# Windowed attention into a gated feed-forward on one core: a new opening list, last hidden slices over whole token tiles, and a first output pass in two spans

## Chip, core and metric

The kernel runs on one core of a Trainium2 chip. The metric is the device time of one execution in microseconds (us), lower is better; where several executions were timed, the median counts. "The profile" is one execution taken with the hardware profiler; its times count from its first instruction. The engines are TensorE (PE in the profile, with its weight loads as PEld), VectorE (DVE), ScalarE (ACT), GpSimd (POOL) and SyncE (SP), and each works through its own instructions in order.

## The reference

```python
# q, k, v: (8 batches, 8 heads, 576 positions, 64), float32
scores = q @ k.T / sqrt(64)
rel = pos[:, None] - pos[None, :]
scores = where((rel >= 0) & (rel < 64), scores, -1e9)
attn = exp(scores - max(scores)); attn = attn / (sum(attn) + 1e-9)
x = (attn @ v).transpose(0, 2, 1, 3).reshape(4608, 512)
h = x @ w_in                      # w_in: 512 x 2048
out = (h * cos(h)) @ w_out        # w_out: 2048 x 512, out: 4608 x 512 float32
```

## The kernel before

The 4608 tokens are cut into nine tiles of 512 (`MT`). For each tile the feed-forward half runs on TensorE as 16 slices of 128 hidden columns (four matmuls of 128x512 per slice, line 445), each followed by a sine on ScalarE (cos h = sin(h + pi/2)) and a product on VectorE that writes the gated slice `gT`; then the output pass (line 607) forms four blocks of 128 tokens, 16 matmuls each. The attention for later batches is pumped in between these matmuls by a plan of due times (`at`, `pump`), so TensorE is given a single long stream.

Tile 0 is different. Nothing can be hidden behind an earlier tile, so everything up to its output pass is issued in the order of one list written out by hand, `FIRST`. A word of it is a step with its arguments and, at the end, the engine (a ScalarE, d VectorE, p GpSimd). The steps are, with p a pair of heads and g a half of the tile's 512 tokens:

- `ld.*` issues a load from the GpSimd queue: q and k of a head pair, v by chunks of 128 positions, `wA`, `wB`, `wC` three pieces of w_in (columns 0 to 512, 512 to 1280, 1280 to 2048), `q1b`, `k1b` the next batch's q and k, `wO`, `wP`, `wR` three pieces of w_out (slices 0 to 8, 8 to 12, 12 to 16). The very first q and k come over the SP queue in float32 and are cast by `cq`, `ck`.
- `io`, `id`, `mkd` build a ramp, the identity and the masks; `mka` casts the masks to bfloat16.
- `tq`, `tk` transpose q and k of a pair on TensorE (line 217); `pq`, `pk` copy them from PSUM to SBUF.
- `s` scores (a mask product, line 318, and eight blocks, line 308), `m` the row maxima (VectorE, line 327), `e` four exponentials (ScalarE, line 342), `i` reciprocals of the sums (VectorE), `n` the normalised weights (GpSimd or VectorE, line 356), `w` their transposes (TensorE, line 365), `c` the copy of these (VectorE).
- `z` copies halves of v to where the shifted blocks want them; `v.a.g` multiplies the weights by v for pairs 2a and 2a+1 (line 402), `x.a.g` copies the result to `xT`.
- `h.i.part` is half of a slice product (line 422): for i from 0 to 7 token half 0, for i from 8 to 15 token half 1, always two hidden slices 2(i mod 8) and 2(i mod 8)+1, with head pairs 0 and 1 in part 0, 2 and 3 in part 1. `sin.i` is its sine (line 428), `g.i` its product (line 433).
- `TQ`, `TK`, `EQ`, `EK` transpose and copy q and k of batch 1. `tb` loads ScalarE's sine table.

The PSUM banks of the scores turn through `S_FIRST`, those of the slices through `H_FIRST`, so `h.0` to `h.4` take the banks of the last five score groups, and `h.4.0` the bank that the last exponentials, `e.3.1`, read. The output pass of tile 0 goes through the hidden slices in three spans for both token blocks e = 0 and 1, so that slices which come late are asked for late:

```python
spans = ((0, 8), (8, 12), (12, 16)) if mt == 0 else ((0, n_ff),)
for lo, hi, e in [(lo, hi, e) for lo, hi in spans for e in range(2)]:
```

Block e = 0 ends in bank O1, which VectorE copies out, block e = 1 in O0, which ScalarE copies out; the next two blocks need the same banks.

Of the kernel before, what the change touches and what calls it, by code (L numbers as in the profile page):

```python
# [9 lines left out]
def _safe_warn(msg, *a, **kw):  # L10
# [6 lines left out]
ALU = mybir.AluOpType  # L17
# [46 lines left out]
def kernel(  # L64
# [9 lines left out]
    nc = tc.nc  # L74
# [5 lines left out]
    n_ff = d_ff // 128  # L80
    MT = 512
# [11 lines left out]
    w_in_sb = const.tile([128, PAIRS, d_ff], BF16, name="w_in")  # L93
# [9 lines left out]
    st = {}  # L103
# [39 lines left out]
    def load_heads(name, b, p0=0, n=PAIRS):  # L143
        if (name, b) not in st:
            st[name, b] = rows[name][b % 2][:, 0:PAIRS * RC * D].rearrange("p (a x) -> p a x", a=PAIRS)
        src = {"q": q, "k": k}[name][b, 2 * p0:2 * p0 + 2 * n]
        nc.gpsimd.dma_start(out=st[name, b][:, p0:p0 + n],
                            in_=src.rearrange("(a h) (p c) d -> (h p) a (c d)", h=2, c=RC))

    def load_first(name):  # L150
        st["f", name] = of = moe.tile([128, 2, d_model], F32, tag="out", name=name + "_f32", bufs=3)
        st["f", name] = of = of.rearrange("p a f -> p (a f)")[:, 0:RC * D]
        nc.sync.dma_start(out=of, in_={"q": q, "k": k}[name][0, 0:2].rearrange("h (p c) d -> (h p) (c d)", c=RC))

# [259 lines left out]
    def first_half(i, part):  # L414

        if part == 0:
            st["h0", i] = bank(H_FIRST[next(h_turn)], "h_ps").rearrange("p (e t) -> p e t", e=2)
        half = slice(MT // 2 * (i // 8), MT // 2 * (i // 8 + 1))
        for e in range(2):
            for ks in range(2 * part, 2 * part + 2):  # L420
                ff = 2 * (i % 8) + e
                nc.tensor.matmul(out=st["h0", i][:, e], lhsT=w_in_sb[:, ks, ff * 128:ff * 128 + 128],  # L422
                                 rhs=st["xT", 0][:, ks, half], start=ks + e == 0, stop=ks == PAIRS - 1,
                                 skip_group_check=True)

    def first_sin(i):
        st["sin", i] = moe.tile([128, MT], F32, tag="sin", name="sin", bufs=4)
# [2 lines left out]
    def first_gate(i):  # L430
        if not st["gT"]:
            st["gT"] = [moe.tile([128, 2, MT], BF16, tag="gT", name="gT", bufs=n_ff // 2 + 2) for _ in range(n_ff // 2)]
        nc.vector.tensor_tensor(out=st["gT"][i % 8][:, :, MT // 2 * (i // 8):MT // 2 * (i // 8 + 1)], in0=st.pop(("h0", i)),
                                in1=st.pop(("sin", i)).rearrange("p (e t) -> p e t", e=2), op=ALU.mult)

    def exp_table():
        nc.scalar.activation(small, small, AF.Exp, scale=0.0)
# [42 lines left out]
    n = n_first  # L480
# [54 lines left out]
    for name in ("q", "k"):  # L535
# [2 lines left out]
    exp_table()  # L538
    loads = {name + str(p): (load_heads, name, 0, p, 1) for name in ("q", "k") for p in range(1, PAIRS)}
    loads.update({f"v{c}": (load_v, 0, c) for c in range(4)})  # L540
    loads.update(wA=(load_w_in, 0, 512), wB=(load_w_in, 512, 1280), wC=(load_w_in, 1280, 2048),
                 q1b=(load_heads, "q", 1), k1b=(load_heads, "k", 1),
                 wO=(load_w_out, 0, 8), wP=(load_w_out, 8, 12), wR=(load_w_out, 12, 16))

# [25 lines left out]
    for mt in range(n_mt):  # L570
        base = mt * T
        gT = st["gT"] = [] if mt else st["gT"]
# [8 lines left out]
        for ff in range(n_ff) if mt else ():  # L581
# [4 lines left out]
            sin = moe.tile([128, MT], F32, tag="sin", name="sin", bufs=4)  # L586
# [3 lines left out]
            e = ff % 2  # L590
# [2 lines left out]
                exp_table()  # L593
            nc.vector.tensor_tensor(out=gt[:, e], in0=h_ps, in1=sin, op=ALU.mult)  # L594
            pump(base + ff)
        spans = ((0, 8), (8, 12), (12, 16)) if mt == 0 else ((0, n_ff),)
        for ms0 in range(0, MT // 128, 2):
            o_sb = moe.tile([128, 2, d_model], F32, tag="out", name="out_sb", bufs=3)
            o_ps = [bank(which, "out_ps") for which in (("O1",) if mt == n_mt - 1 and ms0 else ("O1", "O0"))]
# [1 line left out]
            for lo, hi, e in [(lo, hi, e) for lo, hi in spans for e in range(2)]:  # L601
# [4 lines left out]
                for ff in range(lo, hi):  # L606
                    nc.tensor.matmul(out=o_ps[e], lhsT=gT[ff // 2][:, ff % 2, ms * 128:ms * 128 + 128],  # L607
                                     rhs=w_out_sb[:, ff], start=ff == 0, stop=ff == n_ff - 1)
# [39 lines left out]
```

## Time and profile before

| | us |
|---|---|
| median of 3 runs | 301.59 (301.36 to 302.14) |
| the profiled execution, its own time | 301.93 |
| its span, first to last instruction | 300.1 |

| engine | busy us | share of the span |
|---|---|---|
| TensorE matmuls | 289.9 | 97% |
| TensorE weight loads | 148.1 | 49% |
| VectorE | 221.5 | 74% |
| ScalarE | 234.0 | 78% |
| GpSimd | 171.9 | 57% |

In a timeline row the columns are the start, the time from the first start to the last end of the merged instructions, engine, line, operation and tiles, shapes, how many, and in brackets how long the engine had been idle before and what released it. In a row of a table by stretches the columns are the stretch and its length, the busy time of each engine with its number of instructions, the granted TensorE clock, the share of the DMA engines and GB/s. In a row of the DMA view the last columns are how many transfers, the size of one and the time from issue to landing. The 1.83 us between the profiled time and its span lie outside the first and last instruction.

### The profile page before, as it was taken

To read this page: it belongs to the slowest core of one execution; us is meant where nothing else is said; L and a number is where in the kernel's file an instruction comes from. 1 tells how busy PE (TensorE), PEld (TensorE's weight loads), DVE (VectorE), ACT (ScalarE), POOL (GpSimd) and SP (SyncE) were. 2 spreads that over 40 slices of the span, in tenths; PEclk is the share of its full clock that TensorE was granted. 3 is DMA by queue.
4 is the path that set the end of the run, shared out by engine and by line. 5 is a ranking of instruction groups with operands and counts; after the bars stand their busy time and mean duration, and the time that the engine had idled before them with its cause. 6 is when DMAs were issued, how large, how long until landed. Compare 5 with 4: busy or idle time off the path is not lost.

```text
span 300.1 us, 8095 instructions
## 1 busy us (share of the span) xinstructions
PE 289.9 (97%) x2762; PEld 148.1 (49%) x2762; DVE 221.5 (74%) x852; ACT 234.0 (78%) x781; POOL 171.9 (57%) x202
## 2 busy tenths in 40 slices
PE   3899999999999999999999999999999999999996
PEld 2678744544454445444544454445444444454443
DVE  4899888689867897689678967896789678136701
ACT  4997899778997799879987998799879987016600
POOL 8997356994899278945994689549704610000000
PEclk9999999999999999999999999999999999999999
DMA  8999999999999999999999999999993480011011
GB/s 165 178 198 210 207 163 124 128 146 151 227 178 141 156 225 172 134 163 215 122 159 163 233 156 164 158 232 152 159 188 129 91 175 17 2 72 71 0 70 70
DMA packets 165929, 44.01 MB, mean 147 GB/s; under 512 B 155008, under 2 KB 161152, under 8 KB 165888
## 3 DMA queue, kind: packets, MB, share of 16 engines
q0 software_dynamic: 99360, 18.06, 77.8%
q1 hardware_dynamic: 66384, 25.24, 47.3%
q8 instruction: 21, 0.34, 0.5%
q10 hardware_dynamic: 144, 0.20, 0.2%
q14 instruction: 20, 0.16, 0.2%
HBM read 36.70 MB, written 9.44 MB: 154 GB/s over the span
## 4 chain that ended last, share of the span: by engine, by line
PE 90%; DVE 3%; ACT 2%; POOL 2%; issue 1%; DMA 1%; SPq 0%; DVEq 0%
PE out_ps L607 38%; PE h_ps L445 37%; PE h_ps L422 5%; PE o_ps L383 3%; PE s_ps L308 3%; POOL w L356 1%; ACT e L342 1%; DVE s L331 1%; DMA k_f<-in_k_dram 1%; PE out_ps L457 1%; PE tw_ps L365 1%; PE tk_ps L217 1%; DVE w L356 0%; PE tq_ps L217 0%; POOL v L116 0%
## 5 line engine op out<-in xcount | busy, mean ns | idle before, releaser
L607 PE MATMUL out_ps<-w_out,gT 128*128 128x512 bf16 x560 | 126.3, 379 | 0.5 <-DVE out_sb L116 0.5
L445 PE MATMUL h_ps<-xT,w_in 128*128 128x512 bf16 x512 | 112.0, 379 | 0.2
L594 DVE TENSOR_TENSOR gT<-h_ps,sin 128x512 bf16<-128x512 f32 x128 | 84.9, 688 | 30.1 <-ACT sin L591 30.1
L356 POOL TENSOR_TENSOR w<-e,rden 128x512 bf16<-128x512 f32 (+1 forms) x75 | 73.1, 986 | 54.7 <-DVE rden L349 52.6
L342 ACT ACTIVATE e<-s,negm 128x128 f32<-128x128 f32 x256 | 98.7, 388 | 0.2
L591 ACT ACTIVATE sin<-h_ps 128x512 f32<-128x512 f32 x128 | 73.8, 598 | 27.8 <-PE h_ps L445 26.7
L607 PEld LDWEIGHTS <-gT 128*128 128x128 bf16 x560 | 52.8, 98 | 61.3 <-issue 0.6
L445 PEld LDWEIGHTS <-w_in 128*128 128x128 bf16 x512 | 49.9, 98 | 59.1
L331 DVE CUSTOM_DVE_ANT_0 s<-s_ps,mask 128x128 f32<-128x128 f32 x256 | 57.9, 283 | 1.8 <-PE s_ps L308 1.6
L342 ACT ACTIVATION_READ_ACCUMULATOR e<-s,negm 128x1 f32 x256 | 48.2, 188 | 0.0
L174 POOL DMA_DIRECT2D v<-in_v_dram x40 | 34.1, 869 | 6.8 <-DMA w_out<-in_moe_w_out_dram 4.2
L116 ACT COPY out_sb<-out_ps 128x512 f32<-128x512 f32 (+1 forms) x18 | 10.2, 567 | 25.3 <-PE out_ps L607 19.6
L168 POOL DMA_DIRECT2D k<-in_k_dram x30 | 26.3, 882 | 4.5 <-DMA v<-in_v_dram 4.5
L168 POOL DMA_DIRECT2D q<-in_q_dram x30 | 25.4, 886 | 3.1 <-DMA w_out<-in_moe_w_out_dram 3.1
L116 DVE CAST xT<-o_ps 128x512 bf16<-128x512 f32 x28 | 18.2, 680 | 8.4 <-PE o_ps L383 8.2
L116 DVE COPY out_sb<-out_ps 128x512 f32<-128x512 f32 x18 | 12.3, 682 | 15.1 <-PE out_ps L607 15.1
L349 DVE RECIPROCAL rden<-den 128x4 f32<-128x4 f32 (+1 forms) x80 | 13.6, 171 | 10.2 <-ACT e L342 7.2
L331 DVE DVE_READ_ACCUMULATOR2_ANT negm<- 128x1 f32 x256 | 20.8, 81 | 0.0
L422 PE MATMUL h_ps<-xT,w_in 128*128 128x256 bf16 x128 | 15.5, 273 | 0.0
L422 PEld LDWEIGHTS <-w_in 128*128 128x128 bf16 x128 | 11.9, 98 | 1.5
L116 DVE COPY v<-v 64x1024 bf16<-64x1024 bf16 (+1 forms) x19 | 11.5, 605 | 0.4
L428 ACT ACTIVATE sin<-h_ps 128x512 f32<-128x512 f32 x16 | 9.1, 597 | 2.9 <-PE h_ps L422 2.9
(59 smaller groups left out, 185.8 us busy)
## 6 DMA issues: line engine op xcount, KB each, us to landing
out_dram<-out_sb SPq DMA_DIRECT2D x16, 512.0 KB, 7.8
v<-in_v_dram POOLq DMA_DIRECT2D x32, 128.0 KB, 5.9
q<-in_q_dram POOLq DMA_DIRECT2D x24, 128.0 KB, 9.3
k<-in_k_dram POOLq DMA_DIRECT2D x24, 128.0 KB, 7.8
w_in<-in_moe_w_in_dram POOLq DMA_DIRECT2D x2, 768.0 KB, 11.7
w_out<-in_moe_w_out_dram POOLq DMA_DIRECT2D x1, 1024.0 KB, 13.1
w_out<-in_moe_w_out_dram POOLq DMA_DIRECT2D x2, 512.0 KB, 15.6
wT<-w SPq DMA_TRANSPOSE x60, 5.0
```

Source lines behind the costliest of these rows:

```text
L116: {"a": nc.scalar.copy, "p": nc.gpsimd.tensor_copy}.get(engine, nc.vector.tensor_copy)(out, in_)
L168: nc.gpsimd.dma_start(out=st[name, b][:n, c].rearrange("p (h d) -> p h d", h=H), in_=src.rearrange("h p d -> p h d"))
L174: nc.gpsimd.dma_start(out=vt.rearrange("p (h d) -> p h d", h=H), in_=v[b, :, c * 128:c * 128 + n, :].rearrange("h p d -> p h d"))
L331: nc.vector.tensor_tensor_reduce(out=s[:, u], in0=s_ps[:, u], in1=mask[:, 2 - j % 2 if j else 0], scale=-scale if b else -1.0, scalar=BIG, ...
L342: nc.scalar.activation(e[:, u], s[:, u], AF.Exp, bias=negm[:, u:u + 1], scale=1.0 if n < n_first else -1.0, accum_out=den[:, u:u + 1])
L349: nc.vector.reciprocal(out=rden[:, 0:len(groups[n])], in_=den[:, 0:len(groups[n])])
L356: (nc.gpsimd if engine == "p" else nc.vector).tensor_tensor(out=w[:, 0:u], in0=e[:, 0:u], op=ALU.mult, in1=rden[:, 0:u].unsqueeze(2).to_br ...
L422: nc.tensor.matmul(out=st["h0", i][:, e], lhsT=w_in_sb[:, ks, ff * 128:ff * 128 + 128], rhs=st["xT", 0][:, ks, half], start=ks + e == 0, s ...
L445: nc.tensor.matmul(out=st["h", ff], lhsT=w_in_sb[:, ks, ff * 128:ff * 128 + 128], rhs=st["xT", mt][:, ks], start=start, stop=stop)
L591: nc.scalar.activation(sin, h_ps, AF.Sin, bias=math.pi / 2.0)
L594: nc.vector.tensor_tensor(out=gt[:, e], in0=h_ps, in1=sin, op=ALU.mult)
L607: nc.tensor.matmul(out=o_ps[e], lhsT=gT[ff // 2][:, ff % 2, ms * 128:ms * 128 + 128], rhs=w_out_sb[:, ff], start=ff == 0, stop=ff == n_ff - 1)
```

## The change

Three things change at once.

1. Six of the sixteen steps `h.i` of tile 0 (5, 6, 7, 13, 14, 15) no longer take one token half of two hidden slices, but all 512 tokens of one slice, 10 to 15; sine and product follow. Eight matmuls of 128x256 become four of 128x512 in each. The slices 0 to 9 stay in halves.
2. `wA` and `wB` are no longer columns 0 to 512 and 512 to 1280 for all head pairs, but columns 0 to 1280 for head pairs 0 and 1, and for 2 and 3. The output pass of tile 0 goes in two spans, slices 0 to 8 and 8 to 16.
3. The list `FIRST` is a new one. Engines of some steps change too: the casts `ck` to ScalarE and `mka` to VectorE, the copies `pq.0` and `pk.1` to VectorE, `pk.0` and `pq.1` to ScalarE, `x.1.0` and `c.3.1` to ScalarE, `x.0.1` to VectorE, and others.

```diff
+WHOLE = dict(zip((5, 6, 7, 13, 14, 15), range(10, 16)))
 FIRST = (
-    "ld.q1 ld.k1 io ld.q2 ld.k2 id mkd cq.a ck.d tq.0 ld.q3 tk.0 ld.k3 mka.a pq.0.a tq.1 pk.0.d s.0.0 "
-    "tk.1 s.0.1 pq.1.d ld.v0 tk.2 ld.v1 m.0.0 ld.wA pk.1.a ld.wB m.0.1 pk.2.d s.1.0 ld.v2 ld.v3 e.0.0 "
-    "i.0.0 n.0.0.p tq.2 m.1.0 ld.wC pq.2.d tq.3 s.2.0 tk.3 e.0.1 pq.3.d e.1.0 ld.q1b m.2.0 i.1.0 i.0.1 "
-    "n.1.0.d w.0.0 pk.3.a s.3.0 m.3.0 w.1.0 s.2.1 c.0.0.d s.1.1 c.1.0.d n.0.1.p z.0.p e.2.0 v.0.0 s.3.1 "
-    "e.3.0 i.2.0 m.2.1 e.2.1 m.1.1 n.2.0.p i.3.0 x.0.0.d n.3.0.p m.3.1 i.2.1 w.2.0 e.1.1 n.2.1.p c.2.0.d "
-    "h.0.0 w.3.0 e.3.1 c.3.0.d w.0.1 i.1.1 h.1.0 v.1.0 w.2.1 c.0.1.d n.1.1.p tb x.1.0.d h.2.0 c.2.1.d "
-    "i.3.1 n.3.1.d h.3.0 h.0.1 sin.0 h.1.1 w.1.1 ld.k1b z.1.d w.3.1 z.2.p c.1.1.d sin.1 h.2.1 c.3.1.d "
-    "h.3.1 v.0.1 ld.wO v.1.1 sin.2 h.4.0 h.4.1 g.0 x.0.1.a g.1 h.8.0 x.1.1.d g.2 h.9.0 h.8.1 sin.3 sin.4 "
-    "sin.8 h.9.1 ld.wP h.10.0 g.3 sin.9 h.11.0 h.10.1 sin.10 g.4 h.11.1 h.12.0 g.8 h.12.1 sin.11 h.5.0 "
-    "g.9 sin.12 h.5.1 TQ.0 g.10 sin.5 h.6.0 h.6.1 h.7.0 EQ.0.0.a g.11 g.12 h.7.1 sin.6 g.5 sin.7 TK.0 "
-    "h.13.0 EK.0.0.a h.13.1 EQ.0.1.d TQ.2 sin.13 g.6 g.7 h.14.0 EQ.2.0.a EQ.2.1.a h.14.1 EK.0.1.d TK.2 "
-    "sin.14 h.15.0 g.13 h.15.1 ld.wR EK.2.1.a sin.15 EK.2.0.d g.14 g.15 "
+    "ld.q1 cq.a ld.k1 ld.q2 io ld.k2 id mkd tq.0 ld.q3 ld.k3 ck.a tk.0 mka.d tq.1 pq.0.d pk.0.a pq.1.a "
+    "s.0.0 tk.1 m.0.0 e.0.0 s.0.1 ld.v0 pk.1.d ld.v1 m.0.1 s.1.0 ld.wA tq.2 s.1.1 i.0.0 m.1.0 ld.wB "
+    "pq.2.d tk.2 e.0.1 ld.v2 i.0.1 e.1.0 n.0.0.p ld.v3 n.0.1.p tq.3 m.1.1 pk.2.d tk.3 s.2.0 i.1.0 n.1.0.p "
+    "pk.3.a pq.3.d w.0.0 z.0.p s.3.0 e.1.1 m.2.0 c.0.0.d m.3.0 w.1.0 e.2.0 c.1.0.d ld.wC s.2.1 v.0.0 "
+    "m.2.1 i.1.1 i.2.0 x.0.0.d s.3.1 m.3.1 w.0.1 n.2.0.p e.3.0 n.1.1.p h.0.0 i.3.0 n.3.0.d c.0.1.d h.1.0 "
+    "e.2.1 w.2.0 h.2.0 c.2.0.d w.3.0 w.1.1 i.2.1 h.3.0 c.3.0.d e.3.1 c.1.1.d v.1.0 i.3.1 n.3.1.d h.4.0 "
+    "ld.q1b n.2.1.p x.1.0.a w.2.1 tb ld.k1b h.0.1 c.2.1.d w.3.1 z.1.d sin.0 h.1.1 c.3.1.a g.0 z.2.p h.2.1 "
+    "h.3.1 v.0.1 x.0.1.d ld.wO v.1.1 sin.1 x.1.1.a sin.2 g.1 ld.wP g.2 h.4.1 h.8.0 h.8.1 sin.3 h.9.0 "
+    "h.9.1 h.10.0 g.3 sin.4 sin.8 ld.wR h.10.1 g.4 h.11.0 sin.9 h.11.1 g.8 g.9 h.12.0 h.12.1 sin.10 TQ.0 "
+    "sin.11 g.10 sin.12 h.5.0 g.11 EQ.0.1.a EQ.0.0.d g.12 h.5.1 h.6.0 h.6.1 h.7.0 sin.5 TK.0 h.7.1 sin.6 "
+    "EK.0.0.d h.13.0 h.13.1 g.6 g.5 TQ.2 EK.0.1.a sin.7 sin.13 EQ.2.0.a EQ.2.1.a h.14.0 h.14.1 g.13 TK.2 "
+    "sin.14 g.7 h.15.0 EK.2.1.d EK.2.0.a h.15.1 g.14 sin.15 g.15 "
 )
...
-        for e in range(2):
+        for e in range(1 if i in WHOLE else 2):
             for ks in range(2 * part, 2 * part + 2):
-                ff = 2 * (i % 8) + e
-                nc.tensor.matmul(out=st["h0", i][:, e], lhsT=w_in_sb[:, ks, ff * 128:ff * 128 + 128],
-                                 rhs=st["xT", 0][:, ks, half], start=ks + e == 0, stop=ks == PAIRS - 1,
-                                 skip_group_check=True)
+                ff = WHOLE.get(i, 2 * (i % 8) + e)
+                nc.tensor.matmul(out=st["h0", i].rearrange("p e t -> p (e t)") if i in WHOLE else st["h0", i][:, e],
+                                 lhsT=w_in_sb[:, ks, ff * 128:ff * 128 + 128],
+                                 rhs=st["xT", 0][:, ks] if i in WHOLE else st["xT", 0][:, ks, half],
+                                 start=ks + e == 0, stop=ks == PAIRS - 1, skip_group_check=True)
...
+        if i in WHOLE:
+            to, of = st["gT"][WHOLE[i] // 2][:, WHOLE[i] % 2], of.rearrange("p e t -> p (e t)")
...
-    loads.update(wA=(load_w_in, 0, 512), wB=(load_w_in, 512, 1280), wC=(load_w_in, 1280, 2048),
+    loads.update(wA=(load_w_in, 0, 1280, 0, 2), wB=(load_w_in, 0, 1280, 2, 4), wC=(load_w_in, 1280, 2048),
...
-        spans = ((0, 8), (8, 12), (12, 16)) if mt == 0 else ((0, n_ff),)
+        spans = ((0, 8), (8, 16)) if mt == 0 else ((0, n_ff),)
```

More of the change, by code (lines that the diff above doesn't have):

```diff
@@ L432, in first_gate @@
             st["gT"] = [moe.tile([128, 2, MT], BF16, tag="gT", name="gT", bufs=n_ff // 2 + 2) for _ in range(n_ff // 2)]
-        nc.vector.tensor_tensor(out=st["gT"][i % 8][:, :, MT // 2 * (i // 8):MT // 2 * (i // 8 + 1)], in0=st.pop(("h0", i)),
-                                in1=st.pop(("sin", i)).rearrange("p (e t) -> p e t", e=2), op=ALU.mult)
+        to, of, sin = st["gT"][i % 8][:, :, MT // 2 * (i // 8):MT // 2 * (i // 8 + 1)], st.pop(("h0", i)), st.pop(("sin", i))
+        if i in WHOLE:
+            to, of = st["gT"][WHOLE[i] // 2][:, WHOLE[i] % 2], of.rearrange("p e t -> p (e t)")
+        else:
+            sin = sin.rearrange("p (e t) -> p e t", e=2)
+        nc.vector.tensor_tensor(out=to, in0=of, in1=sin, op=ALU.mult)
     def exp_table():
```

## The prediction

> **What bounds the kernel now.** I read the page first, then a table by stretches, then the timelines of the opening.
>
> ```profile
> span 300.1 us, 8095 instructions
> PE 90%; DVE 3%; ACT 2%; POOL 2%; issue 1%; DMA 1%; SPq 0%; DVEq 0%
> ```
> ```profile
> 5.00:20.50 15.50, 13.64 (x277) 9.76 (x276) 13.05 (x30) 13.21 (x68) 14.67 (x18) 1.00 1.43 182
> 20.50:37.50 17.00, 16.62 (x318) 13.73 (x317) 15.51 (x27) 13.85 (x26) 10.19 (x13) 1.00 1.22 209
> 37.50:58.00 20.50, 19.98 (x225) 9.87 (x224) 17.39 (x109) 19.04 (x85) 14.14 (x18) 1.00 1.38 129
> 58.00:284.00 226.00, 225.71 (x1856) 107.44 (x1855) 171.37 (x678) 184.41 (x600) 129.06 (x145) 1.00 1.33 147
> ```
>
> The chain that ended last is TensorE for 90%. From 58 to 284 us TensorE idles 0.29 us, and the change touches nothing there: what it does to the start of that stretch it does to the end. Before it TensorE idles 1.86 us (5 to 20.5), 0.38 (to 37.5) and 0.52 (to 58). These idles, slow or superfluous matmuls, and the time to the first work are all there is to win.
>
> **The opening, walked through the new list.** These rows give the durations: TensorE, then ScalarE, then VectorE.
>
> ```profile
> 5.33 0.69 PE L217 MATMUL tk_ps<-ident,k 64*64 64x64 bf16 x18 [0.31 <-DVE k L116]
> 6.43 0.61 PE L318 MATMUL s_ps<-mask,ident 128*128 128x256 bf16 x2
> 6.97 0.64 PE L308 MATMUL s_ps<-kT,qT 64*64 64x128 bf16 x8
> 15.37 0.41 PE L308 MATMUL s_ps<-kT,qT 64*64 64x128 bf16 x8
> 19.77 0.40 PE L365 MATMUL tw_ps<-ident,w 128*128 128x128 bf16 x4
> 20.00 1.91 PE L422 MATMUL h_ps<-xT,w_in 128*128 128x256 bf16 x16
> 23.16 0.76 PE L402 MATMUL o_ps<-wT,v 128*64 128x64 bf16 x32
> 23.85 6.29 PE L422 MATMUL h_ps<-xT,w_in 128*128 128x256 bf16 x56
> 36.49 0.41 PE L308 MATMUL s_ps<-kT,qT 64*64 64x128 bf16 x14
> 37.28 0.24 PE L308 MATMUL s_ps<-kT,qT 64*64 64x128 bf16 x2 [0.38 <-ACT sin L428]
> 37.46 2.76 PE L607 MATMUL out_ps<-w_out,gT 128*128 128x512 bf16 x12
> 57.56 13.34 PE L445 MATMUL h_ps<-xT,w_in 128*128 128x512 bf16 x61
> ```
> ```profile
> 3.61 0.67 ACT L116 CAST q<-q_f 128x576 bf16<-128x576 f32 x1 [1.36 <-DMA q_f<-in_q_dram]
> 8.66 0.37 ACT L342 ACTIVATE e<-s_ps,negm 128x128 f32<-128x128 f32 x1
> 10.04 0.39 ACT L342 ACTIVATE e<-s_ps,negm 128x128 f32<-128x128 f32 x1
> 12.82 0.68 ACT L116 COPY kT<-tk_ps 128x576 bf16<-128x576 bf16 x1
> 13.36 0.41 ACT L342 ACTIVATE e<-s_ps,negm 128x128 f32<-128x128 f32 x1
> 18.87 0.49 ACT L342 ACTIVATE e<-s_ps,negm 128x128 f32<-128x128 f32 x1
> 20.15 0.35 ACT L342 ACTIVATION_READ_ACCUMULATOR e<-s_ps,negm 128x1 f32 x1
> ```
> ```profile
> 4.82 0.46 DVE L116 CAST k<-k_f 128x576 bf16<-128x576 f32 x1
> 6.74 0.75 DVE L239 TENSOR_SCALAR qT<-tq_ps 128x576 bf16<-128x576 bf16 x1
> 7.65 0.69 DVE L327 TENSOR_REDUCE negm<-s_ps 128x4 f32<-128x512 f32 x1 [0.16 <-PE s_ps L308]
> 19.88 0.69 DVE L116 CAST xT<-o_ps 128x512 bf16<-128x512 f32 x1 [0.22 <-PE o_ps L402]
> ```
>
> *First scores.* The cast of k goes from VectorE (0.46) to ScalarE, where the same cast of q takes 0.67: `tk.0` starts at 5.53 instead of 5.33, and all behind it on TensorE up to the first scores shifts by 0.20. So `m.0.0` starts at 7.85, and `e.0.0`, which no longer has a copy of kT ahead of it on ScalarE, at 7.85 + 0.69 + 0.02 = 8.56 instead of 8.66. The mask cast, now on VectorE, and the ramp, now one load later on GpSimd, are covered: TensorE is busy with `tk.0` and `tq.1` meanwhile.
>
> *ScalarE's eight groups.* A group takes 1.38 (8.66 to 10.04), the last one 1.63 from its first start to its end (18.87 to 20.50), the copy `pk.3` 0.54 (12.82 to 13.36). New is one wait: `m.0.1` stands behind the copy `pk.1` on VectorE (some 0.7, as the qT copy) and ends near 10.12, 0.2 after ScalarE is free. Sum: 8.56 + 7 x 1.38 + 0.54 + 0.20 + 1.63 = 20.59, against 20.50 now. The other maxima I find in time, by as little as 0.2. VectorE's queue, with 0.61 from the start of a maximum to the next and 0.67 for a copy: `m.0.1` from 9.43 (when `s.0.1` is through), `i.0.0`, `m.1.0` from 10.3, `pq.2`, `i.0.1` at 11.7, `m.1.1` from 11.85, `pk.2` to 13.1, `i.1.0` (after `e.1.0`, whose first row starts at 11.52 and whose sums are there 1.5 later), `pq.3` from 13.3, `m.2.0` from 13.97, ended at 14.65. `e.2.0` can start at 10.14 + 3 x 1.38 + 0.54 = 14.82.
>
> *TensorE up to the second half.* By then the new list has put `h.0.0` to `h.3.0` and `v.1.0` through (ready near 20.4), and waits for `e.3.1` to free the bank of `h.4.0`. From 20.62: five steps `h` of 0.44 (four of the sixteen matmuls that take 20.00 to 21.75 in the row order above; `h.4.0`, `h.0.1` to `h.3.1`), two `w` of 0.23, `v.0.1` and `v.1.1` 0.69: 23.97. Then `h.4.1` to 24.41. `h.8.0` needs `x.0.1`, for which VectorE takes 0.69 after `v.0.1`: 24.55. In the kernel before the same point is 23.85 plus the eight matmuls of `h.4` at 0.111 (6.22 / 56): 24.74. Gain 0.19. `x.1.0`, now on ScalarE between the last exponentials and the sine table, puts `sin.0` off by its 0.6; the product `g.0` is then through near 23.8, before `h.8.0` wants its bank, so this costs nothing as long as TensorE is not more than 0.7 earlier than I have it.
>
> *Fewer matmuls.* 48 of 128x256 at 0.111 become 24 of 128x512 at 0.217 (13.27 / 61): 5.33 - 5.21 = 0.12, whole, because TensorE has no idle there. Sine and product keep their size, so ScalarE and VectorE gain nothing.
>
> *The end of the opening.* Now 14 of the 16 first scores of batch 1 run at 36.49, and the last two wait until 37.28 behind ScalarE: 0.38 idle, up to 0.58 counted by starts. In the new list the last copies of kT (`EK.2.1` now on VectorE, `EK.2.0` on ScalarE) still stand just ahead of `sin.15`. Bounds: the wait stays (0) or goes (-0.58). By my walk the ScalarE copy ends some 0.3 after TensorE asks, so I take -0.30.
>
> **The output pass of tile 0.** In rows of TensorE and VectorE:
>
> ```profile
> 46.02 0.33 PE L365 MATMUL tw_ps<-ident,w 128*128 128x128 bf16 x3
> 46.87 1.02 PE L607 MATMUL out_ps<-w_out,gT 128*128 128x512 bf16 x4 [0.52 <-DVE out_sb L116]
> 52.63 0.69 PE L383 MATMUL o_ps<-wT,v 128*64 128x64 bf16 x32
> ```
> ```profile
> 46.13 0.68 DVE L116 COPY out_sb<-out_ps 128x512 f32<-128x512 f32 x1
> ```
>
> Block e = 0 now ends only four matmuls and a transpose before bank O1 is wanted again, and VectorE, with maxima queued ahead, frees it 0.52 late. With two spans e = 0 ends one group of four earlier: eight matmuls, a transpose, twelve scores and another transpose lie between, about 2.4 us (3 to 4 groups at 0.87 and 0.2 to 0.3 for the rest) instead of 1.2. The copy then ends some 1.1 us before the bank is wanted. Bounds: 0 (another wait takes its place) and -0.68 (46.02 plus 0.17 of transposes to 46.87); I take -0.60, as the neighbours on VectorE keep their distances from TensorE.
>
> **Loads.** The order on the GpSimd queue stays the same, but `wC` and `q1b` are issued some 4 and 6 us later, behind norms and `z.0`. In the trace the transfers are a single backlog that never runs dry, so landings are set by bytes, which stay:
>
> ```profile
> 22.55 2.38 POOL L202 DMA_DIRECT2D w_out<-in_moe_w_out_dram  x3
> ```
> ```profile
> w_out<-in_moe_w_out_dram POOLq DMA_DIRECT2D x1, 1024.0 KB, 13.1
> ```
> ```profile
> w_out<-in_moe_w_out_dram POOLq DMA_DIRECT2D x1, 512.0 KB, 16.6
> ```
> ```profile
> 44.63 1.29 SPq L183 DMA_DIRECT2D v<-v  x2
> ```
> ```profile
> v<-v SPq DMA_DIRECT2D x1, 256.0 KB, 5.6
> ```
>
> The first piece of w_out lands at 22.55 + 13.1 = 35.65, the last (third issue, near 24.2) at 40.8. With the gains above the output pass starts at 37.46 - 0.19 - 0.12 - 0.30 = 36.85, and the two spans ask for the last piece after 16 + 4 matmuls, two score groups and a transpose, at about 42.2: in time by 1.4. The spread of batch 1's v lands at 45.3 + 5.6 = 50.9, and the products that read it, at 52.63 now, come at 52.63 - 1.21 = 51.4: also in time, but this caps any gain at 1.7. w_in's pieces by head pairs cost nothing: part 0 wants `wA`, part 1 `wB`, which is needed at 21.3 only.
>
> **Sum.** -0.19 - 0.12 - 0.30 - 0.60 = -1.21. On the profiled execution 301.93 - 1.21 = 300.72 (span 298.9). That execution stands 0.34 above the median, so for the median I say 301.59 - 1.2 = 300.4.
>
> **A rule against it.** The row of the first mask product shows 0.61 for two matmuls and the eight scores 0.64, later 0.41, while the granted clock stands at 1.00 from the start. The Trainium skill (TensorE: Matmul & The Clock Gate, Part 1: The HAM clock gate) says that TensorE runs at half rate until it has been busy for a window of about 3.4 us, whose phase is free. The durations agree that the start is slow, the clock column does not show it. The new list stretches the hole before `tk.0` and adds waits near 12 to 13 us; by that rule the fast rate could come one window later, which is the third rival.
>
> **The rivals.**
> - *Only the output pass pays.* The list is bound by the same exponentials (20.59 against 20.50), and my 0.2 us margins may be lost: then only about 0.6 stays, 301.0. For it: the loop ScalarE, reciprocal, copies, maximum, ScalarE is close everywhere. Against: TensorE has done two steps `h` more at 20.6.
> - *ScalarE and VectorE slip against each other, and it is slower.* Place: VectorE's queue from `i.1.0` to `m.3.0`. `i.1.0` waits for `e.1.0`, and behind it stand the copy `pq.3`, `m.2.0`, `c.0.0`, `m.3.0`, for which `e.2.0` and `e.3.0` wait. Beyond 0.2 us each delay there passes in full to ScalarE, to `h.4.0`, and to the end; TensorE, in order, can't go around it. The change loses from 1.21 + 0.2 = 1.4 us on. Two groups late by one group (1.38 x 2 = 2.8, less 0.2) make 300.4 + 2.6 = 303.0; one makes 301.6. Against: VectorE is idle for moments, so it can catch up.
> - *The fast rate comes 3.4 us later.* Score groups then cost 0.64 / 0.41 = 1.56 times as much. Of 3.4 us of TensorE work in 10 to 13.5 that is 3.4 x (1 - 0.41 / 0.64) = 1.2, of which the wait for `pk.2` hides about 0.6: 301.0.
> - *All goes well.* The score wait goes entirely and the output pass wins 0.68; the v spread caps it at 1.7: 299.9.
>
> **How the numbers follow.** Forecast 0.44 (its own range 300.0 to 300.8, from the bounds 0 and -0.58, 0 and -0.68), the best case 0.07, the output pass alone 0.20, slipping 0.20, the slow rate 0.09. A measurement tells about 0.3% (0.9 us) from no change: faster means under 300.69, slower over 302.49. The forecast is faster in about 0.42 of its 0.44, the best case wholly: 0.49. The second rival's milder half (0.04) and the two cases near 301.0 are the same, with the forecast's rest: 0.35. Slower 0.16. The range reaches from below the best case to between the two outcomes of slipping: 299.7 to 302.4.
>
> **What would show it.** Right: `e.0.0` near 8.6, `h.4.0` near 20.6 right after the last exponential, `h.8.0` near 24.6, the first L613 output matmul at 36.5 to 37.1, no idle at the first output matmul of the second pair of blocks. Wrong: ScalarE idle among its exponentials, scores or slices waiting for VectorE between 12 and 25 us, an output matmul waiting for w_out, or a products row (L384) waiting for the SP spread.

## The result, and the profile after

| | us |
|---|---|
| kernel after, median of 12 runs | 304.57 (302.27 to 307.24) |
| kernel before, median of 12 runs beside it | 301.94 (301.36 to 302.47) |
| ratio after / before | 1.0082, 95% interval 1.0062 to 1.0103 |
| profiled execution of after, its own time / span | 302.27 / 300.5 |

The change makes the kernel slower by 0.8%. The forecast was 300.4, and the time lies outside its range. The profiled execution is the quickest of the twelve, 2.3 us below their median, so it shows the loss at its smallest.

The kernel after by stretches (length, then busy time and records in brackets for TensorE, its weight loads, VectorE, ScalarE and GpSimd, then the granted clock, DMA share, GB/s):

```profile
5.00:20.50 15.50, 14.22 (x276) 10.14 (x276) 13.50 (x32) 13.34 (x68) 13.53 (x17) 1.00 1.40 187
20.50:37.50 17.00, 16.75 (x305) 11.37 (x301) 15.06 (x25) 14.79 (x27) 10.53 (x14) 1.00 1.22 209
58.00:284.00 226.00, 222.54 (x1825) 106.98 (x1851) 170.51 (x676) 183.80 (x599) 128.41 (x144) 1.00 1.35 146
```

TensorE has 0.58 us more busy time in the first stretch (14.22 against 13.64): the new list leaves it idle less. In the last row it seems to lose 3.2 us, but only 1825 matmul records are there, against 1856 before: most of that is records that are missing, and idle time can't be read from this row. It has to be read from the rows with a named wait. The timeline of TensorE in the kernel after (start, busy time, instruction, and in brackets the idle time before it and what ended it):

```profile
20.66 0.61 PE L423 MATMUL h_ps<-xT,w_in 128*128 128x256 bf16 x4
24.13 5.13 PE L423 MATMUL h_ps<-xT,w_in 128*128 128x256 bf16 x44
36.42 0.42 PE L309 MATMUL s_ps<-kT,qT 64*64 64x128 bf16 x16
36.77 2.76 PE L613 MATMUL out_ps<-w_out,gT 128*128 128x512 bf16 x12
45.50 1.03 PE L613 MATMUL out_ps<-w_out,gT 128*128 128x512 bf16 x3
56.81 13.34 PE L451 MATMUL h_ps<-xT,w_in 128*128 128x512 bf16 x60
86.11 1.01 PE L384 MATMUL o_ps<-wT,v 128*64 128x64 bf16 x52
88.05 0.38 PE L384 MATMUL o_ps<-wT,v 128*64 128x64 bf16 x12 [0.93 <-DMA wT<-w]
88.36 3.84 PE L451 MATMUL h_ps<-xT,w_in 128*128 128x512 bf16 x16
```

and the same place of the kernel before:

```profile
86.86 1.20 PE L383 MATMUL o_ps<-wT,v 128*64 128x64 bf16 x64
88.09 13.97 PE L445 MATMUL h_ps<-xT,w_in 128*128 128x512 bf16 x64
```

Up to the output pass the change does what it was forecast to do: the first output matmul comes at 36.77 (37.46 before), both waits are gone, tile 1's h starts 0.75 earlier. Then, at the products of tile 2, TensorE asks for w's transposes at 86.11, 0.75 earlier than before, and waits 0.93 us for the last of them: tile 2's h starts at 88.36, 0.27 later than before, and the span is 0.4 longer. These transposes are transfers from SyncE's queue (line 369). A list of the transfers issued from 75.3 to 82 us shows them (count, median from issue to landing), in the kernel before and after:

```profile
wT<-w SPq DMA_TRANSPOSE x4, 6.8
```
```profile
wT<-w SPq DMA_TRANSPOSE x4, 7.8
```

On SyncE they stand behind tile 0's two output stores (before, then after; the busy time here is that of issuing):

```profile
71.64 1.04 SPq L465 DMA_DIRECT2D out_dram<-out_sb  x2
76.41 6.40 SPq L368 DMA_TRANSPOSE wT<-w  x4
```
```profile
72.43 1.08 SPq L471 DMA_DIRECT2D out_dram<-out_sb  x2
75.66 6.12 SPq L369 DMA_TRANSPOSE wT<-w  x4
```

Issued 0.75 earlier, they take 1.0 longer, while the stores go out 0.8 later, so that 3.2 us instead of 4.8 lie between the stores and the first transpose. The chain of waits of the kernel after says the same: TensorE is 82% of it (90% before) and w's transposes by DMA 4%:

```profile
PE 82%; DVE 7%; DMA 5%; issue 2%; ACT 1%; POOL 1%; SPq 0%; DVEq 0%; POOLq 0%
PE h_ps L451 36%; PE out_ps L613 34%; PE h_ps L423 4%; DMA wT<-w 4%; PE s_ps L309 3%; DVE s L332 2%; PE o_ps L384 2%; DVE xT L117 1%; PE out_ps L463 1%; DMA k_f<-in_k_dram 1%; DVE negm L328 1%; DVE w L357 1%; ACT e L343 1%; DVE rden L350 1%
```

### The profile page after: what moved, and what is told of

It is laid out like the page before. It is cut to its first block, busy times and chain, and to the rows that moved or that the text cites. A ratio compares the mean times of both kernels' runs of the same rounds, so it can differ in the third digit from the quotient of the medians.

```text
span 300.5 us, 8008 instructions
## 1 busy us (share of the span) xinstructions
PE 287.7 (96%) x2703; PEld 146.0 (49%) x2738; DVE 220.9 (74%) x850; ACT 235.0 (78%) x783; POOL 170.8 (57%) x202
## 4 chain that ended last, share of the span: by engine, by line
PE 82%; DVE 7%; DMA 5%; issue 2%; ACT 1%; POOL 1%; SPq 0%; DVEq 0%; POOLq 0%
PE h_ps L451 36%; PE out_ps L613 34%; PE h_ps L423 4%; DMA wT<-w 4%; PE s_ps L309 3%; DVE s L332 2%; PE o_ps L384 2%; DVE xT L117 1%; PE out_ps L463 1%; DMA k_f<-in_k_dram 1%; DVE negm L328 1%; DVE w L357 1%; ACT e L343 1%; DVE rden L350 1%; POOL w L357 1%
## 5 line engine op out<-in xcount | busy, mean ns | idle before, releaser
L613 PE MATMUL out_ps<-w_out,gT 128*128 128x512 bf16 x542 | 123.5, 379 | 1.7 <-issue 1.3
L597 ACT ACTIVATE sin<-h_ps 128x512 f32<-128x512 f32 x128 | 73.8, 599 | 29.1 <-PE h_ps L451 28.0
L451 PEld LDWEIGHTS <-w_in 128*128 128x128 bf16 x512 | 49.9, 98 | 59.1
L423 PE MATMUL h_ps<-xT,w_in 128*128 128x256 bf16 (+1 forms) x101 | 15.6, 295 | 0.3 <-DVE xT L117 0.2
L343 ACT ACTIVATE e<-s_ps,negm 128x128 f32<-128x128 f32 x32 | 11.3, 439 | 1.3 <-DVE negm L328 1.2
L384 PEld LDWEIGHTS <-v 128*64 128x64 bf16 x512 | 9.1, 112 | 5.2 <-issue 4.7
```

Of the source, the lines that this page charges most:

```text
L343: nc.scalar.activation(e[:, u], s[:, u], AF.Exp, bias=negm[:, u:u + 1], scale=1.0 if n < n_first else -1.0, accum_out=den[:, u:u + 1])
L423: nc.tensor.matmul(out=st["h0", i].rearrange("p e t -> p (e t)") if i in WHOLE else st["h0", i][:, e], lhsT=w_in_sb[:, ks, ff * 128:ff * 1 ...
L451: nc.tensor.matmul(out=st["h", ff], lhsT=w_in_sb[:, ks, ff * 128:ff * 128 + 128], rhs=st["xT", mt][:, ks], start=start, stop=stop)
L597: nc.scalar.activation(sin, h_ps, AF.Sin, bias=math.pi / 2.0)
```

## The experiments

Each had the kernel before timed beside it; the interval is that of the ratio at 95%. "WHOLE" is the change's slices over all tokens.

| kernel | median us (range) | ratio to before |
|---|---|---|
| again: the kernel after | 303.70 (302.49 to 307.0) | 1.0070 (1.0035 to 1.0104) |
| list_only: before + new list | 303.47 (302.72 to 304.97) | 1.0057 (1.0037 to 1.0078) |
| rows_only: before + w_in by head pairs | 301.71 (301.41 to 303.33) | 0.9997 (0.9981 to 1.0013) |
| whole_spans: before + WHOLE + two spans | 302.28 (301.05 to 306.12) | 1.0014 (0.9989 to 1.0038) |
| after_late: after + 1.1 us of matmuls | 302.59 (301.99 to 308.19) | 1.0043 (1.0014 to 1.0073) |
| before_late: before + the same | 303.66 (302.48 to 303.88) | 1.0050 (1.0031 to 1.0068) |
| after_direct: after + 2 groups on TensorE | 301.69 (300.9 to 303.44) | 0.9995 (0.9979 to 1.0011) |
| ws_direct: whole_spans + the same | 301.37 (300.77 to 301.94) | 0.9981 (0.9968 to 0.9994) |
| after_store: after, stores early | 306.47 (304.7 to 307.78) | 1.0139 (1.0103 to 1.0176) |
| before_store | 306.32 (305.25 to 306.83) | 1.0137 (1.0113 to 1.0162) |
| ws_store | 306.56 (305.58 to 309.72) | 1.0164 (1.0126 to 1.0202) |
| ws_direct_store | 307.93 (305.44 to 308.5) | 1.0188 (1.0157 to 1.0219) |
| after_unstored: after, tile 0 not stored | 302.03 (301.33 to 302.61) | 1.0003 (0.9991 to 1.0016) |
| before_unstored | 302.00 (301.64 to 303.31) | 1.0011 (0.9998 to 1.0025) |
| after_half: after, 2nd store behind transposes | 301.29 (300.63 to 303.1) | 0.9983 (0.9969 to 0.9998) |
| ws_half: whole_spans + the same | 301.47 (300.9 to 303.06) | 0.9989 (0.9971 to 1.0006) |
| ws_direct_half: ws_direct + the same | 301.64 (300.94 to 304.41) | 1.0002 (0.9978 to 1.0025) |
| list_half: list_only + the same | 303.66 (302.12 to 305.85) | 1.0043 (1.0023 to 1.0062) |

**1. The parts of the change.** The kernel after once more, and its parts alone, each with its hunks of the change's diff: the new `FIRST`; the pieces of w_in; WHOLE with the two spans under the old list.

> The changed kernel once more, nothing edited. Theory A (the opening is faster, but the DMA transposes of w that tile 2's values product reads are behind a backlog of loads that does not move with TensorE, so TensorE waits for them, more or less long from execution to execution): the first output matmul again near 36.8 us, the product of tile 2's values (L384, near 88 us) again waits for a DMA transpose, by another amount; the longer the execution, the longer that wait or others of its kind; median 304 to 305. Theory B (the new shape of w_in's pieces disturbs the loads): the same here. Theory C (the TensorE clock alone varies): no waits for DMA, matmuls slow.

> The kernel before with the new list alone (w_in's pieces, half slices and three spans as before). Theory A: opening 0.5 us earlier, no total gain; a wait for a transpose of w in tile 1 or 2; 302 to 304. Theory B: nothing of the loads is changed in shape, so the gain of the opening stays: 301.2 to 301.6.

> The kernel before with w_in's first two pieces by rows of head pairs alone. Theory A: TensorE's opening stays, so the phase of TensorE against the loads stays: 301.6 to 302.3, as before. Theory B: 303 to 305 with its spread.

> The kernel before with the six whole slices and the two spans, the old list and w_in's old pieces. Theory A: the output pass of tile 0 ends about 0.7 us earlier and the transposes of w are waited for: no gain, 302 to 304. Theory B: the gain stays: 301.0 to 301.4.

The median of `again` (303.70) is a little below the 304 to 305 that was expected. Its profiled execution (307.0, the slowest of these eight runs) shows the loss at its largest. TensorE's timeline, then stretches of it:

```profile
56.35 3.84 PE L451 MATMUL h_ps<-xT,w_in 128*128 128x512 bf16 x17
70.04 0.64 PE L309 MATMUL s_ps<-kX,qX 64*64 64x128 bf16 x32 [0.35 <-DMA kX<-k]
87.44 0.44 PE L384 MATMUL o_ps<-wT,v 128*64 128x64 bf16 x16 [0.62 <-DMA wT<-w]
89.86 0.54 PE L384 MATMUL o_ps<-wT,v 128*64 128x64 bf16 x12 [1.98 <-DMA wT<-w]
90.33 16.75 PE L451 MATMUL h_ps<-xT,w_in 128*128 128x512 bf16 x64
```
```profile
86.00:90.00 4.00, 1.40 (x60) 1.15 (x61) 1.37 (x3) 2.62 (x5) 3.66 (x6) 0.89 1.72 168
90.00:94.00 4.00, 4.00 (x21) 1.60 (x19) 0.69 (x1) 0.00 (x0) 4.00 (x6) 0.50 2.34 154
94.00:98.00 4.00, 4.00 (x15) 1.64 (x14) 2.50 (x4) 2.55 (x5) 3.81 (x5) 0.75 2.17 166
```

Here tile 1's h starts at 56.35, just the 1.21 before the old 57.56 that the prediction summed up. Then TensorE waits 0.35 for batch 2's transposed k (`kX`) and 0.62 and 1.98 for w's transposes, and after that the clock is granted at half (0.50 from 90 to 94 us): tile 2's 64 matmuls take 16.75 instead of 13.97, another 2.8 us. The four transposes take 8.9 in this execution (7.8 in the first). So late transfers are paid twice here, and the two payments make up the whole loss: tile 2's h starts 2.24 later than in the kernel before and takes 2.8 longer, and the span is 5.1 longer (305.2 against 300.1). The Trainium skill (TensorE: Matmul & The Clock Gate, Part 1: The HAM clock gate) says that TensorE falls back to half rate after an idle window of about 3.4 us; the half rate agrees, the window is looked at below.

The pieces of w_in change nothing, so theory B falls, and the named waits for DMA speak against C. WHOLE with the two spans alone, under the old list, brings the whole gain ahead of tile 1 and loses half of it at the same place: in this execution (301.38, the third quickest of twelve that reach 306.12) tile 2's h starts 0.55 earlier than in the kernel before. TensorE's timeline in whole_spans:

```profile
36.55 1.69 PE L613 MATMUL out_ps<-w_out,gT 128*128 128x512 bf16 x7
56.35 1.90 PE L451 MATMUL h_ps<-xT,w_in 128*128 128x512 bf16 x8
87.23 0.38 PE L384 MATMUL o_ps<-wT,v 128*64 128x64 bf16 x12 [0.57 <-DMA wT<-w]
87.54 2.76 PE L451 MATMUL h_ps<-xT,w_in 128*128 128x512 bf16 x12
```

The new list alone loses 1.6 us and gains nothing, also not ahead of tile 1, against what was expected. Its profiled execution (302.72, the quickest of nine, 0.79 above that of the kernel before) has no wait for a transpose of w at tile 2, but a longer one at the last scores of the opening, 0.89 us instead of 0.38 (TensorE's timeline in list_only):

```profile
37.70 0.24 PE L308 MATMUL s_ps<-kT,qT 64*64 64x128 bf16 x2 [0.89 <-DVE gT L433]
```

That makes tile 1 start 0.42 later than in the kernel before; a wait of 0.21 for kX at 71.53 follows. Experiment 5 comes back to the list.

**2. TensorE put back, or the late transposes taken off the queue.** In two kernels, five overwritten matmuls (5 x 0.217 = 1.1 us) ahead of tile 1's h; in two others, two more of batch 2's head groups transposed on TensorE.

```diff
         def first(...):   # at the first head pair, before its four slices' matmuls
+            for _ in range(5 if (mt, ff) == (1, 0) else 0):
+                nc.tensor.matmul(out=st["h", ff], lhsT=w_in_sb[:, ks, ff * 128:ff * 128 + 128],
+                                 rhs=st["xT", mt][:, ks], start=True, stop=True)
```
```diff
-DIRECT = (0, 1, 2, 3, 4, 5, 8, 9, 16, 17, 26, 27)
+DIRECT = (0, 1, 2, 3, 4, 5, 8, 9, 14, 15, 16, 17, 26, 27)
```

> The kernel after with five extra 128x512 matmuls of TensorE (5 x 0.217 = 1.1 us, overwritten by the group behind them, so the output stays) at the start of tile 1's h, which puts tile 1 and all behind it back to where it lies in the kernel before. Theory A (the transposes by DMA of batch 2's w land late behind loads that do not move with TensorE; an earlier TensorE only waits for them, and long waits lower the clock): the extra work costs less than its 1.1, the median lies at 301.8 to 303.0, not above that of the kernel after, the waits for wT at tile 2's values shrink below 0.5 us in all, and single runs above 305 become rare. Theory C (the clock or the load order of the new list alone, whatever TensorE's phase): the extra work comes on top, 1.1 us above the kernel after, 304.6 to 305.7, with the same spread.

> The kernel before with the same five extra matmuls at the start of tile 1's h, as the price of the extra work where no transfer is late. In the kernel before TensorE takes tile 2's values without a wait, so by theory A the extra work costs up to its whole 1.1 us: 302.7 to 303.1. If it costs nothing (301.6 to 302.1), then a wait for a transfer, at tile 2 or behind it, binds the kernel before too, and anything gained ahead of it was lost from the start. Theory C says nothing against 303.0.

> The kernel after, where the w of two more head groups of batch 2 (pairs 2 and 3, whose transposes by DMA land last ahead of tile 2) is transposed on TensorE: eight more 128x128 transposes (8 x 0.1 = 0.8 us of TensorE) and their copies. Theory A: no wait for wT is left at tile 2's values, no halved clock behind it; the gain of the opening (0.7 to 1.2) stays, less the 0.8: 301.0 to 302.3, with single runs within 1 us of each other. Theory C: nothing changes but the added 0.8, 304 to 305.5.

> The kernel before with the whole-token slices and the two spans of the change, the old list and the old w_in pieces, and the two further head groups of batch 2 transposed on TensorE. Theory A: 1.2 us gained ahead of tile 1 and kept through tile 2, less 0.8 of transposes: 301.0 to 301.8, that is 0 to 0.9 below the kernel before, and no wait for wT at 84 to 90 us. Theory C, or a cost of the copies on VectorE that is larger than the wait: 302.3 or more, no better than the same kernel without the two groups (302.28).

1.1 us of extra work cost the kernel before 1.75 (303.66 against 301.91, more than expected), and the kernel after nothing: 302.59, less than the 303.7 and 304.57 that it took without. So by the medians TensorE only waits away what it gained. The 0.65 above the work itself is the opening's, as far as the profiled execution of before_late (303.82) shows: TensorE waits 0.61 at 6.40 us for the load of the second head pair's q, which it does not in the kernel before, and the second pair of output blocks starts at 47.70 instead of 46.87. But theory A's "shrink below 0.5" failed: in the profiled execution of after_late (305.66, the third slowest of twelve) the waits are as long as ever.

```profile
88.75 0.44 PE L384 MATMUL o_ps<-wT,v 128*64 128x64 bf16 x16 [0.59 <-DMA wT<-w]
91.44 0.38 PE L384 MATMUL o_ps<-wT,v 128*64 128x64 bf16 x12 [2.25 <-DMA wT<-w]
```

The landing is not a fixed time, then: TensorE asks for these products at 87.41, 0.55 later than in the kernel before, and still waits, since the transposes take 9.0 here. So an early TensorE is not all that makes them late; experiments 3 and 4 look for the rest. With two groups fewer by DMA the waits are gone and the loss with them. TensorE's timeline in ws_direct:

```profile
86.02 1.20 PE L384 MATMUL o_ps<-wT,v 128*64 128x64 bf16 x64
87.25 5.12 PE L451 MATMUL h_ps<-xT,w_in 128*128 128x512 bf16 x23
```

No wait, tile 2 starts 0.84 earlier than in the kernel before, and the range narrows to 300.77 to 301.94. The medians are theory A's forecast for both kernels (301.0 to 302.3, 301.0 to 301.8), and C's 304 falls. The runs of after_direct spread over 2.5 us, though, not over the 1 that was expected.

**3. Which traffic makes them late: the stores moved ahead.** Theory A1 blames tile 0's two output stores, A2 the loads of batch 3.

```diff
-        nc.sync.dma_start(out=out[r0:r0 + n * 128]...
+        (nc.sync if mt else nc.scalar).dma_start(out=out[r0:r0 + n * 128]...
-                at(base + T + 6 + ms0 / 2, store, o_sb, mt, ms0, 0, 2)
+                at(base + T + (6 + ms0 / 2 if mt else 1.5 * ms0 - 4), store, o_sb, mt, ms0, 0, 2)
```

> The kernel after, whose two stores of tile 0's output (2 x 512 KB, issued near 72 and 73 us from SyncE and landed near 80 and 81.5, just as the transposes by DMA for tile 2 are issued) are issued from ScalarE's queue near 53 and 57 us instead, where the DMA engines move least. Theory A1 (the stores are what the transposes stand behind): the transposes issued at 75 to 81 us land in 5 to 6.5 us instead of 7 to 9, no wait for wT is left at tile 2's values, and the gain of the opening shows: 300.6 to 301.5. Theory A2 (the transposes stand behind the loads of batch 3's q, k and v, the stores are beside the point): they still take 7 us and more, and the time stays at 302.3 to 304.6. If the earlier stores delay the transposes of batch 2's k, the scores at 70 us wait for kX instead, and the time is that of A2 or worse.

> The kernel before with the same two stores from ScalarE's queue, as the price of the move where no transpose is late. A1 and A2: 301.6 to 302.2, within 0.3 of the kernel before, as no wait of TensorE goes and ScalarE has room for two issues; if it gains over 0.5, a wait behind 90 us that I have not seen goes with it.

> The kernel before with the whole-token slices and the two spans, old list and old w_in pieces, and the early stores. A1: tile 1 starts 1.2 earlier and tile 2 keeps it: 300.5 to 301.0, spread under 1.5. A2: as without the stores' move, 302.3, with single runs up to 306.

> The same with batch 2's groups of pairs 2 and 3 transposed on TensorE as well. A1: the transposes of these groups were no longer late, so they only cost their TensorE time: 0.3 to 0.8 above the same without them, 301.0 to 301.6. A2: they are what keeps the gain: 301.2 to 301.5, 0.8 or more below the same without them.

All four lose 4.4 us and more against the kernel before, the case that only the last sentence of after_store's expectation had: the megabyte now stands ahead of batch 2's k, and tile 1's scores wait. In before_store, TensorE's timeline, the stretch behind that wait, and the transposes issued from 78.7 to 90 us:

```profile
73.72 0.64 PE L308 MATMUL s_ps<-kX,qX 64*64 64x128 bf16 x32 [3.02 <-DMA kX<-k]
```
```profile
73.70:78.00 4.30, 4.28 (x42) 1.87 (x43) 3.86 (x27) 2.76 (x15) 1.16 (x2) 0.63 1.64 157
```
```profile
wT<-w SPq DMA_TRANSPOSE x4, 3.3
```

The transposes did become quick (3.3 instead of 6.8), and no wait for them is left; but they are also issued later, as the loads of this stretch run out (the last of them, issued at 74.17, takes 9.3), so this did not tell A1 from A2. It shows that the place near 53 and 57 us is not free for these bytes, and again the clock drop (0.63) behind a wait of 3.02.

**4. The stores left out, or one of them put behind.** In after_unstored and before_unstored rows 0 to 511 of the output are not written (first diff). In the half kernels the second store is issued behind the last of the four transposes (second diff):

```diff
-            if mt < n_mt - 1:
+            if 0 < mt < n_mt - 1:
                 at(base + T + 6 + ms0 / 2, store, o_sb, mt, ms0, 0, 2)
```
```diff
-                at(base + T + 6 + ms0 / 2, store, o_sb, mt, ms0, 0, 2)
+                at(base + T + (6 if mt or not ms0 else 25.9) + ms0 / 2 * (mt > 0), store, o_sb, mt, ms0, 0, 2)
```

> The kernel after without the two stores of tile 0's output (1 MB; rows 0 to 511 of the output are left out, and SyncE's issues of 71.6 to 73.5). A1: the transposes for tile 2, issued at 75 to 81 us, land in 4 to 6 us, no wait for wT is left, tile 2's h starts 0.7 us before where the kernel before has it, and the time is 300.6 to 301.4 with a spread below 1.5. A2: the transposes still take 7 us and more, and the time is 302.3 to 304.6.

> The kernel before without the same two stores, as the price of the stores where TensorE does not wait: by A1 and A2 301.4 to 302.0, within 0.4 of the kernel before. If it is more than 0.5 faster, stores cost the kernel before too.

> The kernel after, with the second of the two stores (512 KB) put behind the four transposes for tile 2 on SyncE's queue, near 82 us. A1: half the bytes ahead of the transposes, some 1 to 1.5 us less for each (6 to 7 us), waits below 0.3 us: 301.0 to 302.0. A2: 302.3 to 304.6 as before.

> The kernel before with the whole-token slices and the two spans, old list, old w_in pieces, and the second store behind the transposes. A1: tile 1 starts 1.2 earlier and the waits for wT (0.57 in the run without this) go: 300.6 to 301.3, better than the kernel before by 0.6 to 1.3. A2: 302.3.

In after_unstored, the transfers issued from 75.3 to 82 us and TensorE's timeline:

```profile
wT<-w SPq DMA_TRANSPOSE x4, 5.8
```
```profile
86.22 1.20 PE L384 MATMUL o_ps<-wT,v 128*64 128x64 bf16 x64
87.44 4.91 PE L451 MATMUL h_ps<-xT,w_in 128*128 128x512 bf16 x21
```

In after_half:

```profile
wT<-w SPq DMA_TRANSPOSE x4, 7.2
```
```profile
85.95 1.46 PE L384 MATMUL o_ps<-wT,v 128*64 128x64 bf16 x64
87.35 4.92 PE L451 MATMUL h_ps<-xT,w_in 128*128 128x512 bf16 x21
```

Without the stores the transposes take 5.8 instead of 7.8 to 8.9, with one store 7.2. Tile 2's h starts 0.65 and 0.74 earlier than in the kernel before instead of 0.27 later, and the medians fall by 1.7 to 3.3 us to 302.03 and 301.29. In the kernel before, too, they take 4.1 instead of 6.8 without the stores (before_unstored). So A1 holds: with nothing else moved, the stores are what the transposes stand behind. The rest of the traffic counts too, since 5.8 is far from the 2.4 that six of them take late in the kernel after (issued from 229 to 238 us), where nothing else moves:

```profile
wT<-w SPq DMA_TRANSPOSE x6, 2.4
```

The unstored kernel missed its expected 300.6 to 301.4: it is no faster than before_unstored (302.00), nor than after_half, which still writes everything. Why was not settled. ws_half (301.47) missed its 300.6 to 301.3 as well. Its profiled execution (302.71, the second slowest of twelve) has no wait for w at tile 2, but two others ahead of it (TensorE's timeline):

```profile
76.53 1.08 PE L309 MATMUL s_ps<-kX,qX 64*64 64x128 bf16 x40 [0.51 <-DMA kX<-k]
83.43 0.40 PE L366 MATMUL tw_ps<-ident,w 128*128 128x128 bf16 x4 [0.53 <-POOL w L357]
```

So w's transposes are not the only ones without room: a transposed k (kX) is late in `again`, list_only, list_half and ws_half, by 0.21 to 0.51 us. The store put behind, together with the two TensorE groups, brings nothing more:

> The kernel before with the whole-token slices and two spans, batch 2's groups of pairs 2 and 3 transposed on TensorE, and the second of tile 0's stores behind the last transpose for tile 2. If late transposes still cost (A1): 300.6 to 301.2 with a spread below 1, better than the version without the store's move (301.37). If the rest is lost elsewhere, or only in single executions for other reasons: 301.2 to 301.6, no different from it.

301.64 is the second case: what is left is not the transposes for tile 2. In its profiled execution a wait of 0.28 for kX is left, at 69.82.

**5. What the list loses alone.**

> The kernel before with the new list alone, and the second of tile 0's stores behind the transposes for tile 2. If the list's loss goes by the late transposes (A1): 301.6 to 302.2, as the kernel before. If it is the list's own (the opening, or the order of the loads): 303.0 to 303.7, as without the store's move.

The store's move does not help the list alone (303.66, a ratio of 1.0043 against 1.0057 without it, and the intervals overlap), so this loss is another one, and the profiled execution (305.85, the slowest of nine) shows a part of it. TensorE's timeline in list_half, then the stretch from 20.4 to 24:

```profile
20.41 0.61 PE L422 MATMUL h_ps<-xT,w_in 128*128 128x256 bf16 x4 [1.93 <-DMA w_in<-in_moe_w_in_dram]
```
```profile
20.40:24.00 3.60, 3.59 (x37) 2.70 (x38) 2.11 (x4) 0.85 (x3) 3.55 (x5) 0.59 1.19 210
```

The new list asks for `h.2.0`, which reads columns 512 to 767, right after `h.1.0`: near 18.3, where the old list asks for it in the row at 20.00. With w_in still cut by columns these lie in the second piece, which came 1.93 late here, and the clock is at 0.59 behind the wait. In the profiled execution of list_only the same matmuls start without a wait:

```profile
18.34 0.61 PE L422 MATMUL h_ps<-xT,w_in 128*128 128x256 bf16 x4
```

So this piece is just in time in one execution and 1.93 late in another; its load takes 10.5 and 12.6 us. The pieces by head pairs put these columns into the first piece: no profiled execution of a kernel with both shows the wait. Both executions also have the long wait at the last scores of the opening (0.89, and 0.84 in list_half), which no profiled kernel with WHOLE has. The list, the pieces and WHOLE belong together, and list_only is no fair price of the list. A fairer one is after_half against ws_half, which differ by list and pieces: 301.29 and 301.47, nothing that these ranges can tell apart.

Two versions beat both kernels by a little: ws_direct (0.9981, interval to 0.9994) and, only just clear of 1, after_half (0.9983, to 0.9998), some 0.5 us of the 1.2 hoped for.

## Why the prediction was wrong, step by step

- *`h.4.0` and `h.8.0`: right in number, by luck.* `h.4.0` comes at 20.66 (20.62 forecast), the step `h.8.0` at 24.13 + 4 x 0.111 = 24.57 (24.55). But `h.4.0` does not wait for the last exponentials, which were to end at 20.59: ScalarE is through with them at 20.38, and TensorE is still busy with `v.1.0`, behind two waits of its own that the prediction did not have (0.53 at 13.09, 0.38 at 19.21). Nor is the gain of 0.19 shown to be the list's: with the old list `h.8.0` comes at 24.74 in the kernel before, but at 24.54 in rows_only and 24.29 in before_unstored, which order this stretch alike.
- *The term of the first scores came out otherwise:* tk.0 starts at 5.21, not 5.53, and `e.0.0` at 8.38, not 8.56. The cast takes the 0.67 that was forecast; k was there earlier in this execution, so that the cast starts at 4.48 instead of 4.82. With the cast on VectorE, as before, tk.0 starts at 5.09 in rows_only.
- *End of the opening: right, but not by the list.* The score wait is gone wholly (0.38 idle; -0.30 was taken of up to -0.58), first output matmul 36.77 (36.85). It is gone in whole_spans too (36.55), with the old list, and longer in list_only (0.89): it is WHOLE that removes it, not the place of the last copies, by which the prediction reckoned.
- *Output pass: right.* No idle at the second pair of blocks, 45.50 instead of 46.87. From the first output matmul that is 0.68 less, the bound where -0.60 was taken.
- *The sum came out, in part by luck.* Tile 1's h starts at 56.35 in two executions (`again` and whole_spans), 1.21 before the old 57.56, and in the first execution of the kernel after at 56.81. But whole_spans reaches this without the list, whose own term is not seen; rows_only, with the old order, is there at 57.33, 0.23 earlier than the profiled kernel before, since its tk.0 starts at 5.09 instead of 5.33; and a new wait at the products near 52 us, for VectorE's copy wT (0.18), takes back some 0.37.
- *w_in's pieces cost nothing: right* (rows_only 0.9997), but the reason they are there was missed: with the new list they are needed (experiment 5).
- *The step that failed* is the sentence "the change touches nothing there: what it does to the start of that stretch it does to the end". 0.29 us of idle in 226 was read as slack of the transfers too. It says only that TensorE did not wait, not by how much. In the kernel before, the last of the four transposes for tile 2 is issued at 80.88 and takes 6.5, so it lands near 87.4. The products run from 86.86 to 88.06, and the last 12 of the 64, which wait for it in the kernel after, begin near 87.8 (an estimate: 52/64 of 1.20 behind 86.86). So the slack was some 0.5 us, too little for a TensorE that comes 1.2 us earlier. And the landing did not stay: 88.0 in the kernel after (80.13 + 7.9), 89.8 in `again` (80.73 + 9.1). The loads paragraph followed w_out and the spread of v to 52 us and stopped there, and "landings are set by bytes, which stay" was the wrong rule for them: they are issued 0.75 to 1.2 earlier with an earlier TensorE, and how long they take depends on the stores and loads around them (5.8 to 9.0).
- *The rivals.* None was this one, though the first said rightly that the list may win nothing. ScalarE against VectorE did not slip. The fast rate did not come later (scores at 0.41 from 10.88 on, before from 12.09). But the clock did enter, behind 58 us: in `again` 2.60 us of waits cost 2.8 more. The range had no room for that.
- *Open:* why the transposes are late in more executions of the kernel after (median 304.57 and 303.7) than of whole_spans (302.28), which brings TensorE to tile 1 as early. The profiled executions hint at it: between the stores and the first transpose lie 5.0 us in rows_only, 4.8 in the kernel before, 3.5 in whole_spans, 3.2 in the kernel after and 1.9 in `again`, and the transposes take 6.0, 6.8, 7.7, 7.8 and 8.9. What brings the stores later in the kernel after (72.43 and 73.31 against 71.70 in whole_spans) was not tested.

## What to carry to other kernels

A stretch in which the bounding engine never idles says nothing on how near each transfer is to being late: before counting a gain at the start of such a stretch to its end, take for each transfer in it issue, landing and first use, and see whether the smallest slack is larger than the gain. Where a transfer's issue follows the engine, an earlier engine may issue it into other traffic; look for large transfers that nobody waits for, such as stores, on the same queue ahead of it, and put them behind. And when a reordered list is tried alone, its data and its slices must be cut for it, or the trial measures the wrong cut. An old time taken from one profiled execution is uncertain by what that execution drew: here 0.2 us, by the landing of one load.

## What the runs showed of the hardware

Behind a wait of TensorE the granted clock can fall. It stood at 0.50 in the four us behind waits of 0.62 and 1.98 (`again`), at 0.63 behind 3.02 (before_store) and at 0.59 behind 1.93 (list_half), but stayed at 1.00 behind 0.59 and 2.25 in after_late, where tile 2's 64 matmuls take 13.99:

```profile
88.00:92.00 4.00, 1.16 (x42) 0.80 (x35) 1.40 (x4) 2.31 (x3) 3.67 (x6) 1.00 1.69 160
92.00:96.00 4.00, 4.00 (x20) 1.85 (x19) 1.80 (x4) 1.88 (x4) 4.00 (x5) 1.00 1.80 146
```

So the length of the wait alone does not decide it. The Trainium skill's idle window of about 3.4 us, in the section named above, is longer than the 1.93 us that sufficed here.

A transpose of w by DMA takes 2.4 us where nothing else moves, 3.3 to 5.8 beside loads alone (before_store, before_unstored, after_unstored), and 5.9 to 9.0 with both of tile 0's stores ahead of it (before_late to after_late).
